# Turning q in 32x32 blocks on VectorE and scoring in 32x64 array tiles, in a fused low-rank attention and max-of-three FFN kernel

## Chip, cores and metric

One core of one Trainium2 chip runs the whole problem in one launch. The metric is the device time in microseconds of that core; three runs of the kernel before give a median of 399.84 us (399.8 to 400.65).

## What is computed

The inputs q, k, v are float32 of shape 8 x 8 x 1024 x 64 (batch, head, token, d); E and F are 64 x 1024. The FFN weights w1, w2, w3 are 512 x 768, w_out is 768 x 512. The output is float32, 8192 x 512.

```python
k_proj = np.einsum('ks,bhsd->bhkd', E, k)
v_proj = np.einsum('ks,bhsd->bhkd', F, v)
scores = np.matmul(q, k_proj.transpose(0, 1, 3, 2)) / np.sqrt(64)
scores = scores - np.max(scores, axis=-1, keepdims=True)
attn = np.exp(scores)
attn = attn / (np.sum(attn, axis=-1, keepdims=True) + 1e-09)
attn_out = np.matmul(attn, v_proj)
x = attn_out.transpose(0, 2, 1, 3).reshape(8 * 1024, 8 * 64)
h = np.maximum(np.maximum(x @ w1, x @ w2), x @ w3)
out = h @ w_out
```

The 1024 tokens are projected to 64 rows before the scores, so a score matrix is 1024 x 64 per head.

## The kernel before

Everything runs in bf16 with float32 sums. Token 8p + si of a batch lies in partition p at place si, so `q_t`, `k_t` and `v_t` are [128, head, 8, 64]. They are loaded with a cast by GpSimd's queue (`load`, L81), two buffers each.

The FFN works on half batches of 512 tokens (`ch`), 16 in all. One `l1` call (L176) is four matmuls of 128x128 by 512 columns into one of four rotating PSUM banks (0 to 3), and an eviction: ScalarE copies w1's product (L182), VectorE takes the maximum with w2's (L184) and with w3's (L186). So the same bank comes round four groups later, and the eviction of a group must be done by then. 18 such groups make one half batch; four `down` groups of six matmuls (L188) of the half batch before are put between them after groups 2, 5, 8 and 11.

The attention of the next batch is spread among these groups by a list of slots written out by hand: `attention` (L111) returns pairs of a slot number and a step, and `tick` (L457), called after every group, starts the steps that are due. In batches 2 to 7 the steps are: `kv` at slot 2 (the projections of k and v, 16 matmuls into bank 4), `scores(0)` at 10, `scores(1)` at 15, `sums` at 20, two reciprocals, and the two halves of the product with v at 25 and 30. For batch 1 the list is written out at L452, denser: `kv` at 20, `scores(0)` at 25, `scores(1)` at 28. Batch 0 has its own code and the change leaves its work alone.

The steps that matter here:

- After `kv`, the projected k is copied from PSUM to `kp2` twice over, once by ScalarE (L122) and once by VectorE (L123), so that a crossbar transpose on the Sync queue (L167) gives `kpT` with d in partitions 0 to 63 and again in 64 to 127. Two copies of the projected v follow on ScalarE (L125) and VectorE (L126). The four copies run one after another: each waits for the one before it on the other engine.
- q has to come with d on partitions too. For batches 2 to 7 two crossbar transposes per batch on the Sync queue do this (`q_turn`, L95): a partition of `qT` is (parity of the token, d). For batch 1 TensorE does it: `q_pe1` (L296), 32 transposes into PSUM and four copies out, at slots 22 and 24.
- `scores(u)` (L128) makes eight matmuls of 64 rows by 64 columns with 512 moving columns, four at a time in four 64x64 tiles of the array, and then two exponentials of 1024 elements per partition on ScalarE (L138).
- `load_behind_turn` (L89) lets GpSimd read one element of `kpT` before it issues the next loads, so the loads follow the turn of k.

Of the kernel before, what the change touches and what calls it, by code (L numbers as in the profile page):

```python
# [16 lines left out]
def kernel(ctx: ExitStack, tc: tile.TileContext, q, k, v, E, F, w1, w2, w3, w_out, out):  # L17
# [37 lines left out]
    xT = [T([P, NCT, 2, 512], BF16, f"xT{i}") for i in range(3)]  # L55
# [32 lines left out]

    def load_behind_turn(b, order="qkv"):  # L89

        nc.gpsimd.tensor_copy(out=seen, in_=kpT[(b - 1) % NB][:, 0, 0:1])
        for c in order:
            load(b, *{"q": (q, q_t), "k": (k, k_t), "v": (v, v_t)}[c])

    def q_turn(b, hs):  # L95
        nc.sync.dma_start_transpose(
            out=qT[b % NB][:, hs].rearrange("p h s t -> p (h s) t"),
            in_=q_t[b % NB][:, hs].rearrange("p h si d -> p (h si d)"),
        )


# [9 lines left out]
    def attention(b, turn):  # L111
        i = b % NB

        def kv():
            for si in range(SI):
                nc.tensor.matmul(out=ps[0:KP, AB, :], lhsT=eT[:, si, :], rhs=k_t[i][:, :, si, :],  # L116
                                 start=(si == 0), stop=(si == SI - 1))
                nc.tensor.matmul(out=ps[KP:P, AB, :], lhsT=fT[:, si, :], rhs=v_t[i][:, :, si, :],  # L118
                                 start=(si == 0), stop=(si == SI - 1))
            kv_k = ps[0:KP, AB, :].rearrange("p (h d) -> p h d", d=D)  # L120
            kv_v = ps[KP:P, AB, :].rearrange("p (g u dd f) -> p u g f dd", u=2, f=2, dd=HD)
            nc.scalar.copy(out=kp2[i][:, :, 0, :], in_=kv_k)  # L122
            nc.vector.tensor_copy(out=kp2[i][:, :, 1, :], in_=kv_k)  # L123
            turn(i)
            nc.scalar.copy(out=vp2[i][KP:P], in_=kv_v[:, 1])  # L125
            nc.vector.tensor_copy(out=vp2[i][0:KP], in_=kv_v[:, 0])  # L126

        def scores(u):  # L128
            for gg in range(2):
                g = 2 * u + gg  # L130
                for par in range(2):
                    r = slice(par * D, (par + 1) * D)
                    for col in range(2):
                        h = HEAD[2 * g + col]
                        nc.tensor.matmul(out=ps[col * KP:(col + 1) * KP, AB + 2 * gg + par, :],  # L135
                                         lhsT=kpT[i][r, h, :], rhs=qT[i][r, h, :, :], start=True, stop=True)
# [12 lines left out]
        def sums():  # L149
            quads(lambda rows, g: ones[rows, :])  # L150
            for u in range(2):
                nc.scalar.activation(out=lns[u], in_=ps[:, AB + 2 * u:AB + 2 * u + 2, :], func=AF.Ln)  # L152

        def recip(u):
            nc.scalar.activation(out=rinv[u], in_=lns[u], func=AF.Exp, scale=-1.0)  # L155

        def av(half):
            quads(lambda rows, g: vp2[i][rows, g, half, :])
            for u in range(2):
                nc.vector.tensor_tensor(out=xT[b % 3][:, 2 * u + half, :, :], in0=ps[:, AB + 2 * u:AB + 2 * u + 2, :],  # L160
                                        in1=rinv[u].rearrange("p (c n) -> p c n", c=2), op=ALU.mult)

        return [(2, kv), (10, lambda: scores(0)), (15, lambda: scores(1)), (20, sums),
                (21, lambda: recip(0)), (22, lambda: recip(1)), (25, lambda: av(0)), (30, lambda: av(1))]

    def turn_dma(i):
        nc.sync.dma_start_transpose(out=kpT[i], in_=kp2[i].rearrange("p h c d -> p (h c d)"))  # L167


    state = {"f": 0, "n": 0}  # L170
# [5 lines left out]
    def l1(b, ch, c, jt, i):  # L176
        bank = fbank()
        for ct in range(NCT):
            nc.tensor.matmul(out=ps[:, bank, :], lhsT=w_sb[i][:, ct, jt * P:(jt + 1) * P],  # L179
                             rhs=xT[b % 3][:, ct, ch, :], start=(ct == 0), stop=(ct == NCT - 1))  # L180
        if i == 0:
            nc.scalar.copy(out=h1s[jt % 2], in_=ps[:, bank, :])  # L182
        elif i == 1:
            nc.vector.tensor_tensor(out=m12[jt % 2], in0=ps[:, bank, :], in1=h1s[jt % 2], op=ALU.max)  # L184
        else:
            nc.vector.tensor_tensor(out=hT[c % 2][:, jt, :], in0=ps[:, bank, :], in1=m12[jt % 2], op=ALU.max)  # L186
# [45 lines left out]
    def k_proj0(g):  # L232
        for si in range(SI):
            for u in range(2):
                nc.tensor.matmul(out=ps[u * D:(u + 1) * D, 2, g * KP:(g + 1) * KP], lhsT=k_t[0][:, HEAD[2 * g + u], si, :],
                                 rhs=eT[:, si, :], start=(si == 0), stop=(si == SI - 1))
        nc.vector.tensor_copy(out=kpT[0][:, g, :], in_=ps[:, 2, g * KP:(g + 1) * KP])

    def v_proj0(g, bank):
        for si in range(SI):  # L240
# [5 lines left out]
    def scores0(ch, g, bank):  # L246
        for u in range(2):
            rows = slice(u * D, (u + 1) * D)
            nc.tensor.matmul(out=ps[u * KP:(u + 1) * KP, bank, :], lhsT=kpT[0][rows, g, :],  # L249
                             rhs=qT[0][rows, 4 * ch + g, :, :], start=True, stop=True)  # L250
# [21 lines left out]
    def q_up0():  # L272
# [4 lines left out]
                                     rhs=ident, start=True, stop=True)  # L277
        for j in range(2):
            (nc.vector.tensor_copy if j else nc.scalar.copy)(
                out=qT[0][:, 4 + 2 * j:6 + 2 * j].rearrange("p h s t -> p (h s t)"),  # L280
                in_=ps[:, 4 + 2 * j:6 + 2 * j, :].rearrange("p b n -> p (b n)"))

    def scores_up0():
# [5 lines left out]
    def av_up0():  # L289
# [6 lines left out]
    def q_pe1(hh):  # L296
        for h in range(4 * hh, 4 * hh + 4):
            for sp in range(SI // 2):
                o = (h % 2) * 512 + sp * P
                nc.tensor.transpose(out=psb[:, AB + (h % 4) // 2, o:o + P],  # L300
                                    in_=q_t[1][:, h, 2 * sp:2 * sp + 2, :].rearrange("p s d -> p (s d)"), identity=ident)
        for j in range(2):
            (nc.vector.tensor_copy if j else nc.scalar.copy)(
                out=qT[1][:, 4 * hh + 2 * j:4 * hh + 2 * j + 2].rearrange("p h s t -> p (h s t)"), in_=psb[:, AB + j, :])

    def warmup(n, bank):
        for _ in range(n):
# [47 lines left out]
    def q_turn0(g):  # L355
        for n in range(4):
            nc.tensor.transpose(out=psb[:, 4 + g, n * P:(n + 1) * P],
                                in_=q_0[:, n, 2 * g:2 * g + 2, :].rearrange("p h d -> p (h d)"), identity=ident)
        nc.vector.tensor_copy(out=qT[0][:, g].rearrange("p s t -> p (s t)"), in_=psb[:, 4 + g, 0:512])

    def q_cast0(g):
        if g > 1:
# [85 lines left out]
    for b in range(B):  # L448
        groups = attention(b + 1, turn_dma) if b + 1 < B else []
        if b == 0:  # L450
            g1 = [g for _, g in groups]
            groups = [(9, scores_up0), (12, lambda: sums0(1, 4)), (20, g1[0]), (22, lambda: q_pe1(0)), (24, lambda: q_pe1(1)), (25, g1[1]), (28, g1[2]),  # L452
                      (31, g1[3]), (32, g1[4]), (33, g1[5]), (34, g1[6]), (36, g1[7])]
        slot = 0
        gi = 0
# [1 line left out]
        def tick():  # L457
# [79 lines left out]
```

The softmax here doesn't subtract the row's maximum and nothing guards it: scores larger than these inputs give would overflow.

## Time and profile before

| what | value |
|---|---|
| three runs, median | 399.84 us |
| the profiled execution, its own time | 399.92 us |
| its span in the trace | 398.1 us |
| TensorE matmul busy | 392.5 us, 99% of the span |
| VectorE busy | 186.9 us, 47% |
| ScalarE busy | 166.0 us, 42% |
| GpSimd busy | 71.6 us, 18% |
| granted TensorE clock | 1.00 |
| mean DMA rate | 135 GB/s |
| crossbar transposes of q (L96) | 12 |
| crossbar transposes of k (L167) | 7 |

All times in the sections below are microseconds from the start of the span. The time of the profiled execution is 1.8 us longer than its span: the rest lies around the first and last instruction. A line such as "L123 DVE CAST kp<-ps 64x512" says source line, engine, operation, what is written from what, and partitions by elements; then come the count, the busy time, the mean in nanoseconds of one, and the idle time of the engine just before it with what ended that. Matmuls overlap in the array, so a matmul's mean time is a latency and not its share of the engine; what a group of matmuls costs is the distance between the starts of what stands before and behind it.

### The profile page before, as it was taken

What the parts mean: (1) busy time and instruction counts of PE and PEld (TensorE: products, weight loads), DVE (VectorE), ACT (ScalarE), POOL (GpSimd) and SP (SyncE); (2) the same over time, 40 slices, a digit from 0 to 9 for tenths busy, and PEclk for the clock granted to TensorE, in tenths of its full rate; (3) what the DMA queues carried; (4) which work ended last, traced back from release to release, by engine and by line L of the source; (5) the groups of instructions that cost most, each with busy time, mean ns of one, the idle gap of its engine ahead of it and who ended that gap; (6) DMA issues with size and microseconds to landing.
All of it is one profiled execution on the core that took longest, in us unless ns stands there. A gap on an engine that the chain in (4) does not pass through costs nothing.

```text
span 398.1 us, 6013 instructions
## 1 busy us (share of the span) xinstructions
PE 392.5 (99%) x2432; PEld 170.0 (43%) x2432; DVE 186.9 (47%) x269; ACT 166.0 (42%) x249; POOL 71.6 (18%) x110
## 2 busy tenths in 40 slices
PE   8999999999999999999999999999999999999996
PEld 4444443444444444444444444444444444444443
DVE  3347355453834365443843266342654338433441
ACT  3414457347225642347223662245522472222222
POOL 6452140150003300060000600033010000000000
PEclk9999999999999999999999999999999999999999
DMA  8999979999912998169920999129992111102022
GB/s 225 206 209 206 207 172 195 240 162 185 191 54 72 187 197 174 34 116 186 239 95 13 173 197 213 54 67 180 220 131 63 55 53 54 53 7 100 1 107 105
DMA packets 62667, 53.73 MB, mean 135 GB/s; under 512 B 30512, under 2 KB 57648, under 8 KB 62640
## 3 DMA queue, kind: packets, MB, share of 16 engines
q0 software_dynamic: 31776, 43.52, 53.8%
q1 hardware_dynamic: 30032, 8.92, 15.3%
q10 hardware_dynamic: 832, 0.92, 0.7%
q8 instruction: 19, 0.31, 0.3%
q14 instruction: 8, 0.07, 0.0%
HBM read 57.15 MB, written 16.78 MB: 186 GB/s over the span
## 4 chain that ended last, share of the span: by engine, by line
PE 95%; DMA 2%; DVE 1%; ACT 0%; POOL 0%; issue 0%; POOLq 0%; DVEq 0%
PE ps L179 59%; PE ps L203 19%; PE ps L116 3%; PE ps L145 3%; PE ps L407 2%; DMA k_t<-in_k_dram 2%; PE ps L135 2%; PE ps L398 1%; PE ps L216 1%; PE ps L308 1%; PE ps L229 1%; DVE xT L160 1%; PE ps L249 1%; PE ps L300 0%; PE ps L242 0%; PE ps L196 0%
## 5 line engine op out<-in xcount | busy, mean ns | idle before, releaser
L179 PE MATMUL ps<-xT,w_sb 128*128 128x512 bf16 x1080 | 246.3, 379 | 0.0
L179 PEld LDWEIGHTS <-w_sb 128*128 128x128 bf16 x1080 | 103.2, 98 | 132.1 <-issue 12.0
L184 DVE TENSOR_TENSOR m<-ps,h1s 128x512 f32<-128x512 f32 x90 | 62.2, 691 | 143.8 <-PE ps L179 124.5
L203 PE MATMUL ps<-wo_sb,hT 128*128 128x512 bf16 x354 | 85.5, 379 | 0.0
L182 ACT COPY h1s<-ps 128x512 f32<-128x512 f32 x90 | 52.8, 587 | 66.8 <-PE ps L179 66.5
L205 ACT COPY o_acc<-ps 128x512 f32<-128x512 f32 x59 | 34.6, 587 | 97.8 <-PE ps L203 97.8
L210 POOL DMA_DIRECT2D out_dram<-o_acc x28 | 20.1, 720 | 271.1 <-ACT o_acc L205 271.1
L186 DVE TENSOR_TENSOR hT<-ps,m 128x512 bf16<-128x512 f32 x90 | 62.3, 692 | 13.7 <-PE ps L179 5.2
L203 PEld LDWEIGHTS <-hT 128*128 128x128 bf16 x354 | 33.6, 98 | 44.1 <-issue 5.4
L160 DVE TENSOR_TENSOR xT<-ps,rinv 128x1024 bf16<-128x1024 f32 x28 | 32.9, 1218 | 7.8 <-PE ps L145 7.8
L138 ACT ACTIVATE pT<-ps 128x1024 bf16<-128x1024 f32 x28 | 27.1, 1022 | 13.3 <-PE ps L135 13.3
L87 POOL DMA_DIRECT2D v_t<-in_v_dram x21 | 15.3, 750 | 4.0 <-DMA q_t<-in_q_dram 2.0
L152 ACT ACTIVATE lns<-ps 128x1024 f32<-128x1024 f32 x14 | 13.6, 1022 | 1.9 <-PE ps L145 1.9
L155 ACT ACTIVATE rinv<-lns 128x1024 f32<-128x1024 f32 x14 | 14.2, 1061 | 0.0
L116 PE MATMUL ps<-k_t,eT 128*64 128x512 bf16 x56 | 13.4, 382 | 0.0
L118 PE MATMUL ps<-v_t,fT 128*64 128x512 bf16 x56 | 13.4, 382 | 0.0
L87 POOL DMA_DIRECT2D q_t<-in_q_dram x14 | 10.6, 767 | 3.2 <-DMA wo_sb<-in_moe_w_out_dram 1.1
L87 POOL DMA_DIRECT2D k_t<-in_k_dram x14 | 10.5, 762 | 2.2 <-ACT o_acc L445 1.2
L407 PE MATMUL ps<-xT,w_sb 128*128 128x512 bf16 x48 | 10.9, 379 | 0.0
L123 DVE CAST kp<-ps 64x512 bf16<-64x512 f32 x7 | 4.8, 683 | 12.6 <-ACT kp L122 12.6
L308 PE MATMUL ps<-warm 128*128 128x512 bf16 x26 | 9.4, 469 | 1.2 <-DVE ones L340 1.2
L122 ACT CAST kp<-ps 64x512 bf16<-64x512 f32 x7 | 4.1, 580 | 14.1 <-PE ps L118 14.1
(85 smaller groups left out, 155.5 us busy)
## 6 DMA issues: line engine op xcount, KB each, us to landing
out_dram<-o_acc POOLq DMA_DIRECT2D x30, 512.0 KB, 3.3
q_t<-in_q_dram POOLq DMA_DIRECT2D x15, 512.0 KB, 8.5
k_t<-in_k_dram POOLq DMA_DIRECT2D x14, 512.0 KB, 13.4
v_t<-in_v_dram POOLq DMA_DIRECT2D x18, 256.0 KB, 17.6
v_t<-in_v_dram POOLq DMA_DIRECT2D x7, 512.0 KB, 16.8
w_sb<-in_moe_w_dram POOLq DMA_DIRECT2D x4, 384.0 KB, 10.1
k_t<-in_k_dram POOLq DMA_DIRECT2D x4, 256.0 KB, 8.4
w_sb<-in_moe_w_dram POOLq DMA_DIRECT2D x4, 192.0 KB, 9.6
```

The costliest lines, as they stand in the source:

```text
L87: nc.gpsimd.dma_start(out=dst[b % NB][:, slots], in_=sv[:, heads])
L116: nc.tensor.matmul(out=ps[0:KP, AB, :], lhsT=eT[:, si, :], rhs=k_t[i][:, :, si, :], start=(si == 0), stop=(si == SI - 1))
L138: nc.scalar.activation(out=pT[:, 2 * u + gg, :, :], in_=ps[:, AB + 2 * gg:AB + 2 * gg + 2, :], func=AF.Exp, scale=scale)
L160: nc.vector.tensor_tensor(out=xT[b % 3][:, 2 * u + half, :, :], in0=ps[:, AB + 2 * u:AB + 2 * u + 2, :], in1=rinv[u].rearrange("p (c n) -> ...
L179: nc.tensor.matmul(out=ps[:, bank, :], lhsT=w_sb[i][:, ct, jt * P:(jt + 1) * P], rhs=xT[b % 3][:, ct, ch, :], start=(ct == 0), stop=(ct == ...
L182: nc.scalar.copy(out=h1s[jt % 2], in_=ps[:, bank, :])
L184: nc.vector.tensor_tensor(out=m12[jt % 2], in0=ps[:, bank, :], in1=h1s[jt % 2], op=ALU.max)
L186: nc.vector.tensor_tensor(out=hT[c % 2][:, jt, :], in0=ps[:, bank, :], in1=m12[jt % 2], op=ALU.max)
L203: nc.tensor.matmul(out=ps[:, bank, :], lhsT=hT[c % 2][:, jt, tt * P:(tt + 1) * P], rhs=wo_sb[:, jt, :], start=(jt == 0), stop=(jt == NJT - 1))
L205: nc.scalar.copy(out=o[:, tt, :], in_=ps[:, bank, :])
L210: nc.gpsimd.dma_start(out=dst[:, tt - 1:tt + 1, :], in_=o[:, tt - 1:tt + 1, :])
L407: nc.tensor.matmul(out=ps[:, bank, :], lhsT=w_sb[i][:, ct, jt * P:(jt + 1) * P], rhs=xT[0][:, ct, 0, :], start=(ct == 0), stop=(ct == NCT ...
```

## The change

q of batches 1 to 7 is turned by VectorE: `q_flip(b, g)` transposes two heads in 32x32 blocks, with two neighbouring bf16 values of d taken as one float32 word, [128, 512] words at a time, four calls per batch. Within a band of 32 partitions this puts the pair of d on the partition, and leaves the token in its band: partition 32r + j holds d pair j of the tokens of band r, with the two halves of the pair (f) side by side along the row.

The scores follow from that: for each pair of heads, 16 matmuls of 32 rows (d pairs of one band) by 64 columns with 256 moving columns, in eight 32x64 tiles at once, two passes f = 0 and 1 summed in PSUM; the moving operand steps over every second bf16 value. Four banks (one per band) hold 256 columns of each head pair. `kpT` becomes [128, head, f, 64] with the 32 d pairs repeated in the four bands, so `kp2` is filled with four repeats: ScalarE copies heads 0 to 3 and VectorE heads 4 to 7, 64 x 1024 elements each, and the crossbar transpose of k is twice as large. Neither the crossbar nor TensorE turns q of batches 1 to 7 any more. The exponential writes its result in token order, so the output's rows are addressed with a partition holding four neighbouring tokens per half batch. `xT` has two buffers in place of three.

```diff
-    qT = [T([P, H, SI // 2, P], BF16, f"qT{i}") for i in range(NB)]
-    kp2 = [T([KP, H, 2, D], BF16, f"kp2_{i}") for i in range(NB)]
-    kpT = [T([P, H, KP], BF16, f"kpT{i}") for i in range(NB)]
+    qT = [T([P, H, SI * D], BF16, f"qT{i}") for i in range(NB)]
+    kp2 = [T([KP, H, 2, 4, D // 2], BF16, f"kp2_{i}") for i in range(NB)]
+    kpT = [T([P, H, 2, KP], BF16, f"kpT{i}") for i in range(NB)]
...
-    out_v = out.rearrange("(b p sp par) m -> b par p sp m", p=P, sp=SI // 2, par=2)
+    out_v = out.rearrange("(b p ch t) m -> b ch p t m", p=P, ch=2, t=4)
...
-    def q_turn(b, hs):
-        nc.sync.dma_start_transpose(
-            out=qT[b % NB][:, hs].rearrange("p h s t -> p (h s) t"),
-            in_=q_t[b % NB][:, hs].rearrange("p h si d -> p (h si d)"),
+    def q_flip(b, g):
+        hs = slice(2 * g, 2 * g + 2)
+        nc.vector.transpose(
+            out=qT[b % NB][:, hs].bitcast(FP32).rearrange("p h n -> p (h n)"),
+            in_=q_t[b % NB][:, hs].rearrange("p h si d -> p (h si d)").bitcast(FP32),
         )
...
-            kv_k = ps[0:KP, AB, :].rearrange("p (h d) -> p h d", d=D)
+            kv_k = ps[0:KP, AB, :].rearrange("p (h dd f) -> p h dd f", dd=HD, f=2)
...
-            nc.scalar.copy(out=kp2[i][:, :, 0, :], in_=kv_k)
-            nc.vector.tensor_copy(out=kp2[i][:, :, 1, :], in_=kv_k)
+            for r in range(2):
+                (nc.vector.tensor_copy if r else nc.scalar.copy)(
+                    out=kp2[i].rearrange("k h f r dd -> k h r dd f")[:, 4 * r:4 * r + 4],
+                    in_=kv_k[:, 4 * r:4 * r + 4, None].to_broadcast([KP, 4, 4, HD, 2]))
...
-                for par in range(2):
-                    r = slice(par * D, (par + 1) * D)
-                    for col in range(2):
-                        h = HEAD[2 * g + col]
-                        nc.tensor.matmul(out=ps[col * KP:(col + 1) * KP, AB + 2 * gg + par, :],
-                                         lhsT=kpT[i][r, h, :], rhs=qT[i][r, h, :, :], start=True, stop=True)
+                for f in range(2):
+                    for r in range(4):
+                        rows = slice(r * HD, (r + 1) * HD)
+                        for col in range(2):
+                            h = HEAD[2 * g + col]
+                            nc.tensor.matmul(out=ps[col * KP:(col + 1) * KP, AB + r, gg * 256:(gg + 1) * 256],
+                                             lhsT=kpT[i][rows, h, f, :],
+                                             rhs=qT[i][rows, h].rearrange("p (n f) -> p n f", f=2)[:, :, f],
+                                             start=(f == 0), stop=(f == 1), tile_position=(r * HD, col * KP))
             for gg in range(2):
-                nc.scalar.activation(out=pT[:, 2 * u + gg, :, :], in_=ps[:, AB + 2 * gg:AB + 2 * gg + 2, :],
-                                     func=AF.Exp, scale=scale)
+                nc.scalar.activation(
+                    out=pT[:, 2 * u + gg].rearrange("p ch (t r n) -> p r (ch t) n", t=4, r=4),
+                    in_=ps[:, AB:AB + 4, gg * 256:(gg + 1) * 256].rearrange("p r (si n) -> p r si n", si=SI),
+                    func=AF.Exp, scale=scale)
...
-            groups = [(9, scores_up0), (12, lambda: sums0(1, 4)), (20, g1[0]), (22, lambda: q_pe1(0)), (24, lambda: q_pe1(1)), (25, g1[1]), (28, g1[2]),
+            groups = [(9, scores_up0), (12, lambda: sums0(1, 4)), (20, g1[0]),
+                      (22, lambda: q_flip(1, 0)), (23, lambda: q_flip(1, 1)), (25, g1[1]), (26, lambda: q_flip(1, 2)),
+                      (27, lambda: q_flip(1, 3)), (28, g1[2]),
                       (31, g1[3]), (32, g1[4]), (33, g1[5]), (34, g1[6]), (36, g1[7])]
...
-                if slot == 28:
-                    q_turn(2, slice(0, H // 2))
                 return
-            if b == 1 and slot == 3:
-                q_turn(2, slice(H // 2, H))
+            if b == 1 and slot in (4, 5, 6, 7):
+                q_flip(2, slot - 4)
             if b + 2 < B:
                 if slot == 9:
                     load_behind_turn(b + 2)
-                if slot == 18:
-                    q_turn(b + 2, slice(0, H // 2))
-                if slot == 27:
-                    q_turn(b + 2, slice(H // 2, H))
+                if slot in (32, 34, 36, 38):
+                    q_flip(b + 2, slot // 2 - 16)
```

More of the change, by code (lines that the diff above doesn't have):

```diff
@@ L49 @@
     q_t = [T([P, H, SI, D], BF16, f"q_t{i}") for i in range(NB)]
-    qT = [T([P, H, SI // 2, P], BF16, f"qT{i}") for i in range(NB)]
-    kp2 = [T([KP, H, 2, D], BF16, f"kp2_{i}") for i in range(NB)]
-    kpT = [T([P, H, KP], BF16, f"kpT{i}") for i in range(NB)]
+    qT = [T([P, H, SI * D], BF16, f"qT{i}") for i in range(NB)]
+    kp2 = [T([KP, H, 2, 4, D // 2], BF16, f"kp2_{i}") for i in range(NB)]
+    kpT = [T([P, H, 2, KP], BF16, f"kpT{i}") for i in range(NB)]
     vp2 = [T([P, NPAIR, 2, D // 2], BF16, f"vp2_{i}") for i in range(NB)]
     pT = T([P, NPAIR, 2, 512], BF16, "pT")
-    xT = [T([P, NCT, 2, 512], BF16, f"xT{i}") for i in range(3)]
+    xT = [T([P, NCT, 2, 512], BF16, f"xT{i}") for i in range(2)]
     lns = [T([P, 1024], FP32, f"lns{i}") for i in range(2)]
@@ L89, in load_behind_turn @@
     def load_behind_turn(b, order="qkv"):
-        nc.gpsimd.tensor_copy(out=seen, in_=kpT[(b - 1) % NB][:, 0, 0:1])
+        nc.gpsimd.tensor_copy(out=seen, in_=kpT[(b - 1) % NB][:, 0, 0, 0:1])
         for c in order:
             load(b, *{"q": (q, q_t), "k": (k, k_t), "v": (v, v_t)}[c])
-    def q_turn(b, hs):
-        nc.sync.dma_start_transpose(
-            out=qT[b % NB][:, hs].rearrange("p h s t -> p (h s) t"),
-            in_=q_t[b % NB][:, hs].rearrange("p h si d -> p (h si d)"),
+    def q_flip(b, g):
[3 more added lines that the diff above has]
+            in_=q_t[b % NB][:, hs].rearrange("p h si d -> p (h si d)").bitcast(FP32),
         )
@@ L159, in av @@
             for u in range(2):
-                nc.vector.tensor_tensor(out=xT[b % 3][:, 2 * u + half, :, :], in0=ps[:, AB + 2 * u:AB + 2 * u + 2, :],
+                nc.vector.tensor_tensor(out=xT[b % 2][:, 2 * u + half, :, :], in0=ps[:, AB + 2 * u:AB + 2 * u + 2, :],
                                         in1=rinv[u].rearrange("p (c n) -> p c n", c=2), op=ALU.mult)
@@ L166, in turn_dma @@
     def turn_dma(i):
-        nc.sync.dma_start_transpose(out=kpT[i], in_=kp2[i].rearrange("p h c d -> p (h c d)"))
+        nc.sync.dma_start_transpose(out=kpT[i].rearrange("p h f k -> p (h f) k"), in_=kp2[i].rearrange("k h f r dd -> k (h f r dd)"))
     state = {"f": 0, "n": 0}
@@ L179, in l1 @@
             nc.tensor.matmul(out=ps[:, bank, :], lhsT=w_sb[i][:, ct, jt * P:(jt + 1) * P],
-                             rhs=xT[b % 3][:, ct, ch, :], start=(ct == 0), stop=(ct == NCT - 1))
+                             rhs=xT[b % 2][:, ct, ch, :], start=(ct == 0), stop=(ct == NCT - 1))
         if i == 0:
@@ L236, in k_proj0 @@
                                  rhs=eT[:, si, :], start=(si == 0), stop=(si == SI - 1))
-        nc.vector.tensor_copy(out=kpT[0][:, g, :], in_=ps[:, 2, g * KP:(g + 1) * KP])
+        nc.vector.tensor_copy(out=kpT[0][:, g, 0, :], in_=ps[:, 2, g * KP:(g + 1) * KP])
     def v_proj0(g, bank):
@@ L248, in scores0 @@
             rows = slice(u * D, (u + 1) * D)
-            nc.tensor.matmul(out=ps[u * KP:(u + 1) * KP, bank, :], lhsT=kpT[0][rows, g, :],
-                             rhs=qT[0][rows, 4 * ch + g, :, :], start=True, stop=True)
+            nc.tensor.matmul(out=ps[u * KP:(u + 1) * KP, bank, :], lhsT=kpT[0][rows, g, 0, :],
+                             rhs=qT[0][rows, 4 * ch + g, :], start=True, stop=True)
     def exp0(ch, g, bank):
@@ L279, in q_up0 @@
             (nc.vector.tensor_copy if j else nc.scalar.copy)(
-                out=qT[0][:, 4 + 2 * j:6 + 2 * j].rearrange("p h s t -> p (h s t)"),
+                out=qT[0][:, 4 + 2 * j:6 + 2 * j].rearrange("p h n -> p (h n)"),
                 in_=ps[:, 4 + 2 * j:6 + 2 * j, :].rearrange("p b n -> p (b n)"))
@@ L293, in av_up0 @@
         norm0(1, 1, 4, (0, 1))
[L296 to L304, printed above, removed]
     def warmup(n, bank):
@@ L358, in q_turn0 @@
                                 in_=q_0[:, n, 2 * g:2 * g + 2, :].rearrange("p h d -> p (h d)"), identity=ident)
-        nc.vector.tensor_copy(out=qT[0][:, g].rearrange("p s t -> p (s t)"), in_=psb[:, 4 + g, 0:512])
+        nc.vector.tensor_copy(out=qT[0][:, g], in_=psb[:, 4 + g, 0:512])
     def q_cast0(g):
```

## Prediction, before the changed kernel ran

> **What bounds the kernel now.** I read the page first, for the engine that is always busy and the chain that ended last; its second line of part 2 and the chain's engine line:
>
> ```profile
> PE   8999999999999999999999999999999999999996
> ...
> PE 95%; DMA 2%; DVE 1%; ACT 0%; POOL 0%; issue 0%; POOLq 0%; DVEq 0%
> ```
>
> From slice 2 to the last but one TensorE never rests, and it is 95% of the chain. So a microsecond on TensorE counts whole, and one elsewhere counts only if TensorE comes to wait for it. Next the groups by form (count, busy us, mean ns, idle before):
>
> ```profile
> L135 PE MATMUL ps<-qT,kpT 64*64 64x512 bf16 x112 | 8.8, 388 | 0.0
> L123 DVE CAST kp<-ps 64x512 bf16<-64x512 f32 x7 | 4.8, 683 | 12.6 <-ACT kp L122 12.6
> L122 ACT CAST kp<-ps 64x512 bf16<-64x512 f32 x7 | 4.1, 580 | 14.1 <-PE ps L118 14.1
> L300 PE MATMUL ps<-ident,q_t 128*128 128x128 bf16 x32 | 2.1, 219 | 0.4 <-DVE vp L126 0.4
> ```
>
> L123 waits for L122, not for TensorE: the copies of k are one chain. Third, the chain in order of time where batch 1 is prepared (start, us, what):
>
> ```profile
> 49.74 0.59 ACT kp L122
> 50.34 0.02 issue
> 50.36 0.69 DVE kp L123
> 51.05 0.02 issue
> 51.08 0.38 ACT vp L125
> 51.45 0.02 issue
> 51.48 0.44 DVE vp L126
> 51.91 0.04 issue
> 51.95 1.05 PE ps L300 x16
> 53.01 1.73 PE ps L179 x8
> 54.73 0.89 PE ps L300 x16
> 55.63 0.86 PE ps L179 x4
> 56.49 0.56 PE ps L135 x8
> ```
>
> This is the one place where TensorE turns q, and it waits here for the copies. Fourth, the timeline behind `kv` of a later batch (start, us, engine):
>
> ```profile
> 165.05 0.58 ACT L122 CAST kp<-ps 64x512 bf16<-64x512 f32 x1 [2.15 <-PE ps L118]
> 165.67 0.68 DVE L123 CAST kp<-ps 64x512 bf16<-64x512 f32 x1 [1.73 <-ACT kp L122]
> 166.38 0.37 ACT L125 CAST vp<-ps 64x256 bf16<-64x256 f32 x1 [0.75 <-DVE kp L123]
> 166.78 0.43 DVE L126 CAST vp<-ps 64x256 bf16<-64x256 f32 x1 [0.43 <-ACT vp L125]
> ...
> 167.24 0.69 DVE L186 TENSOR_TENSOR hT<-ps,m 128x512 bf16<-128x512 f32 x1
> ```
>
> VectorE's eviction L186 stands behind the four copies and ends at 167.93. Its bank is taken again four groups later, by a group whose first matmul started at 168.81: 0.88 of slack. Last, the turns (duration min/median/max, ns):
>
> ```profile
> L96 SPq DMA_TRANSPOSE qT<-q_t x12: 2034/8246/10241, 71.9 to 283.1; - x12
> L167 SPq DMA_TRANSPOSE kpT<-kp x7: 1194/1196/1272, 51.1 to 306.5; - x7
> ```
>
> The crossbar turns of q run under full TensorE: nobody waits for them.
>
> **What the Trainium skill says.** Three places of the Trainium skill bear on this. "TensorE: Matmul & The Clock Gate", Part 3 (The mechanism): matmuls in different tiles start about 4 ns apart and run together. The trace agrees: four L135 starts lie 3 to 4 ns apart (172.793 to 172.803), the next four 0.240 later. "TensorEngine Tiling (Array Packing)", Key Properties: changing the tiling mode drains the array. The trace shows it: 0.309 in place of 0.216 between starts on entry, 0.308 on leaving. "SBUF — State Buffer" (SBUF cachelines): 16-byte lines are read at full rate with at least two hits each. The new moving operand, every second bf16, has four hits. The only strided moving operand before is L348 (284 to 328 ns against L235's 196): its weights are strided by 16 bytes as well. Their load takes 217 ns against 113, and a matmul ends 112 to 113 ns after its load in both lines, so I put the slowness on the weights. No run here separates the two.
>
> **The change, part by part.** All is summed against the profiled execution, 399.92 (span 398.1 and 1.8 around it), within 0.1 of the 399.84 median.
>
> *Scores, 14 groups, all on the path.* From the last matmul before a group to the first behind it is 0.867, against 0.216 between plain neighbours: a group costs 0.651. That is two switches of 0.093, two rounds of 0.216, and some 0.033 of first weights and spacing. After: 32 matmuls in eight tiles are four rounds of 256 columns. A round of 512 is 0.216 and one of 128 is 0.056 (the L300 starts), so 256 is 0.109: 4 x 0.109 + 0.186 + 0.05 = 0.67. The number of columns per tile, 1024, is unchanged. 14 x 0.02 = **+0.3**. Bounds: -0.2 if the spacing is hidden; +6.1 if the strided operand streams at half rate (0.109 more in each of 56 rounds).
>
> *Copies of k.* Each now covers 64x1024. ScalarE: L138 does 1024 from PSUM in 1022 ns, L122 does 512 in 580: +0.44. VectorE: L160 does 1024 from PSUM in 1218, L123 683: +0.54. The order of the built program keeps VectorE's copy waiting for ScalarE's, so the chain grows by 0.98. Against 0.88 of slack plus a few hundredths for the semaphore, TensorE stalls 0.16 in each of batches 3 to 7: **+0.8**. Scattered two-byte writes could double the copies (another 2.2 in each batch, +11 at most; I hold that unlikely, as L126 reads at a stride of two for no extra); zero if the slack just holds.
>
> *Batch 2, prepared in batch 1.* No `down` groups stand here, the slack is 0.5 (L186 ends 79.70, the bank is wanted at 80.21): a stall of 0.48. Four transposes at slots 4 to 7 then stand before L184 and L186. A transpose of 128x512 words is unknown: nearest row L343, a cast of 128x512 SBUF to SBUF, 628 ns; I take 0.65, and 1.2 as the upper bound (half rate). Group 9 of that half batch (counted from 0, as all here) then waits 0.2 for its bank. **+0.7** (0 to 2.5).
>
> *Batch 1.* Removed: 32 transposes x 0.056 = 1.79, and the wait before them, 51.37 to 51.95, 0.58; two copies of 1.01 on ScalarE and two of 0.69 on VectorE. Without them TensorE would reach `scores(0)` at 54.1. But VectorE now has: k copy to 52.0, v copy to 52.9, L184 to 53.6, L186 to 54.3, two transposes to 55.7. Group 8 waits 0.5 for L184's bank, and `scores(0)` for the second transpose. The turn of k, twice as large, starts at 52.05; L167 lands 2.6 after its issue, 3.6 in batch 1. The q turn of the same 16 blocks issues in 2.03, 0.84 longer, and lands 5.0 after. I take 3.4 (2.6 to 5.2): kpT at 55.5. So `scores(0)` starts at 55.7 against 56.42 before, -0.7; at slots 26 and 27 the last transpose ends near 59.5 where the second half of `scores(1)` wants it at 59.15, +0.35. Net **-0.4** (-1.3 to +1.6).
>
> *At nothing:* the transposes at slots 32 to 38. VectorE has 1.4 of evictions in 3.9 there, 2.7 with two transposes; the banks keep about one us of slack, even at 1.2 each. Removing 12 crossbar turns frees the Sync queue, which had nothing urgent behind them. The larger turn of k has from 167.35 to 172.8 for its 3.4; GpSimd's loads behind it (L91) keep their slot. q of batch 2 landed at 74.3; a us later is still before VectorE's first transpose near 80.7. The exponential stays at 1024 elements; output packets only grow.
>
> Sum: 399.92 + 0.3 + 0.8 + 0.7 - 0.4 = **401.3**.
>
> **Rivals.** (a) *Faster.* The turn of q on TensorE in batch 1 is the only TensorE work that goes. Its price is 2.37; it decides if kpT and two transposes are there by 54.6 and the slack behind `kv` holds: then 399.92 - 2.37 + 0.5 + 0.3 = 398.4. Against it: VectorE's own queue, 55.7 by the rows above. (b) *Cancel.* The slack of 0.88 just covers the copies and batch 2's transposes are short: 399.92 + 0.3 + 0.3 - 0.4 = 400.1. (c) *Strided operand at half rate:* 401.3 + 6.1 = 407.4; for it L348's slowness, against it the equal distance from load to end. (d) *VectorE's transposes at half rate:* batch 1 to +1.1, batch 2 to +2.2: 404.3. That the change doesn't do what it says is excluded by the built program: no q turn on Sync or TensorE is left, 28 transposes stand on VectorE.
>
> **How the numbers follow.** Forecast 0.45 (400.7 to 403); (a) 0.13; (b) 0.17; (c) 0.12; (d) 0.13. Same means within 0.2%, 0.8 us, about what a measurement of this kernel tells from no change. Faster is (a), 0.13; same (b), 0.17; slower the rest, 0.70. The range 398.9 to 405.5 leaves out (c), the far part of (a) and the doubled copies. The forecast's own range lies inside.
>
> **What would show it.** The start-to-start cost of a scores group: 0.67, and its rounds 0.109; 0.22 would be (c). Means of the two copies of k: 1.02 and 1.22. Means of the transposes: 0.65. TensorE waiting for VectorE's L186 behind each `kv` by 0.1 to 0.2, 0.5 in batch 1. `scores(0)` of batch 1 near 55.7, with the DVE transpose as the last to arrive. I am wrong if the copies overlap, if the turn of k takes over 4, or if a group costs over 0.8.

## The result, and the profile after

| kernel | median, us | range, us |
|---|---|---|
| before | 400.02 | 399.8 to 400.65 |
| changed | 465.72 | 464.5 to 466.24, and once 560.19 |

The changed kernel takes 1.1634 times as long as the one before (95% interval 1.1601 to 1.1666): 66 us more, where 1.4 were forecast and the range ended at 405.5. One of its four executions ran at a mean granted clock of 0.73 and took 560.19 us, so the median above is of the other three, at 0.94, and the profile shown here is of a further execution of the same kernel, at 465.38 us (span 463.6).

The page first, in the order in which the prediction read it: TensorE's busy tenths and its granted clock in 40 slices, and the engines' shares of the chain that ended last.

```profile
PE   8999579579993999859997599957999489999996
...
PEclk9999869979997999959999799996999979999999
...
PE 78%; DVE 10%; ACT 8%; DMA 2%; issue 1%; POOL 0%; DVEq 0%; POOLq 0%
```

TensorE was solid from slice 2 on; now it has seven holes of one or two slices, and the clock falls in the same places. VectorE and ScalarE, 1% of the chain before, are 18% of it. The groups by form (count, busy us, mean ns, idle before) name the lines:

```profile
L126 DVE CAST kp<-ps 64x1024 bf16<-64x1024 f32 x7 | 32.6, 4657 | 41.3 <-ACT kp L126 41.3
L126 ACT CAST kp<-ps 64x1024 bf16<-64x1024 f32 x7 | 32.8, 4686 | 14.2 <-PE ps L121 14.2
L99 DVE STREAM_TRANSPOSE qT<-q_t 128x512 f32<-128x512 f32 x28 | 19.3, 695 | 0.0
```

The two copies of k take 4.66 and 4.69 us each, against 0.68 and 0.58 before. The turn of q, the new operation, has 0.695. The waits of TensorE (engine, line, what it waited for: us in total, times, longest):

```profile
PE ps L189 <- DVE hT L196: 43.8, 6, 7.5
PE ps L189 <- DVE m L194: 7.5, 1, 7.5
```

That is 51.3 us, one wait in each of the seven batches that are prepared beside the FFN. L189 and L196 are the matmul and the eviction that were L179 and L186 before. The timeline behind `kv` of one batch shows what the eviction stood behind:

```profile
135.73 4.69 ACT L126 CAST kp<-ps 64x1024 bf16<-64x1024 f32 x1 [2.15 <-PE ps L121]
...
140.45 4.66 DVE L126 CAST kp<-ps 64x1024 bf16<-64x1024 f32 x1 [5.83 <-ACT kp L126]
145.14 0.37 ACT L130 CAST vp<-ps 64x256 bf16<-64x256 f32 x1 [4.72 <-DVE kp L126]
...
145.54 0.42 DVE L131 CAST vp<-ps 64x256 bf16<-64x256 f32 x1 [0.43 <-ACT vp L130]
145.99 0.69 DVE L196 TENSOR_TENSOR hT<-ps,m 128x512 bf16<-128x512 f32 x1
...
146.74 1.86 PE L189 MATMUL ps<-xT,w_sb 128*128 128x512 bf16 x4 [7.09 <-DVE hT L196]
```

It is the chain that the prediction drew: ScalarE's copy, VectorE's copy, the two copies of v, then L196, whose bank TensorE needs. Only it now takes 10.95, from 135.73 to 146.68, where it took 2.88. The last line holds a second loss: four matmuls of L189 in 1.86 us, where four of L179 took 1.04 in the kernel before, at full clock:

```profile
164.92 1.04 PE L179 MATMUL ps<-xT,w_sb 128*128 128x512 bf16 x4
```

The busy times of each engine by stretch say so too (stretch; us; PE, PEld, DVE, ACT, POOL busy; PEclk; DMA share; GB/s):

```profile
140.00:147.00 7.00, 0.26 (x1) 0.10 (x1) 6.09 (x4) 1.85 (x4) 0.00 (x0) 0.77 0.09 14
147.00:154.00 7.00, 6.95 (x53) 2.79 (x53) 1.71 (x3) 1.82 (x3) 1.40 (x3) 0.74 0.33 87
```

In the first stretch TensorE does nothing until 146.74. In the second it is busy throughout, at a mean clock of 0.74: (1 - 0.74) x 7 / 0.5 = 3.6 us of it at half.

### The profile page after: what moved, and what is told of

It reads as the page before. It is cut to its first block, busy times and chain, and to the rows that moved or that the text cites. A ratio compares the mean times of both kernels' runs of the same rounds, so it can differ in the third digit from the quotient of the medians.

```text
span 558.2 us, 6574 instructions
## 1 busy us (share of the span) xinstructions
PE 504.7 (90%) x2686; PEld 197.5 (35%) x2736; DVE 229.9 (41%) x295; ACT 192.6 (34%) x247; POOL 66.5 (12%) x110
## 4 chain that ended last, share of the span: by engine, by line
PE 84%; DVE 8%; ACT 6%; issue 1%; DVEq 0%
PE ps L189 51%; PE ps L213 17%; ACT kp L126 6%; DVE kp L126 6%; PE ps L119 3%; PE ps L155 2%; PE ps L406 2%; PE ps L141 2%; PE ps L307 2%; PE ps L226 1%; PE ps L397 1%; DVE hT L196 1%; DVE vp L131 1%; PE ps L239 1%; PE ps L259 0%
## 5 line engine op out<-in xcount | busy, mean ns | idle before, releaser
L189 PE MATMUL ps<-xT,w_sb 128*128 128x512 bf16 x1043 | 320.2, 467 | 47.0 <-DVE hT L196 37.1
L189 PEld LDWEIGHTS <-w_sb 128*128 128x128 bf16 x1080 | 120.1, 113 | 232.5 <-issue 230.9
L194 DVE TENSOR_TENSOR m<-ps,h1s 128x512 f32<-128x512 f32 x90 | 62.1, 691 | 194.6 <-PE ps L189 187.1
L213 PE MATMUL ps<-wo_sb,hT 128*128 128x512 bf16 x348 | 113.0, 475 | 0.8 <-issue 0.2
L196 DVE TENSOR_TENSOR hT<-ps,m 128x512 bf16<-128x512 f32 x90 | 61.8, 686 | 35.4 <-PE ps L189 34.9
L220 POOL DMA_DIRECT2D out_dram<-o_acc x28 | 15.2, 544 | 406.0 <-ACT o_acc L215 394.6
L213 PEld LDWEIGHTS <-hT 128*128 128x128 bf16 x354 | 39.9, 116 | 63.6 <-issue 63.2
L126 DVE CAST kp<-ps 64x1024 bf16<-64x1024 f32 x7 | 32.6, 4658 | 45.2 <-ACT kp L126 45.2
L126 ACT CAST kp<-ps 64x1024 bf16<-64x1024 f32 x7 | 32.8, 4687 | 19.0 <-PE ps L121 19.0
L99 DVE STREAM_TRANSPOSE qT<-q_t 128x512 f32<-128x512 f32 x28 | 19.3, 694 | 0.0
L119 PE MATMUL ps<-k_t,eT 128*64 128x512 bf16 x56 | 16.8, 454 | 0.0
L121 PE MATMUL ps<-v_t,fT 128*64 128x512 bf16 x56 | 16.7, 455 | 0.0
L165 ACT ACTIVATE rinv<-lns 128x1024 f32<-128x1024 f32 x14 | 14.2, 1060 | 0.0
L406 PE MATMUL ps<-xT,w_sb 128*128 128x512 bf16 x46 | 13.7, 462 | 0.3 <-issue 0.2
## 6 DMA issues: line engine op xcount, KB each, us to landing
w_sb<-in_moe_w_dram POOLq DMA_DIRECT2D x4, 384.0 KB, 10.2
```

The costliest lines, as they stand in the source:

```text
L126: (nc.vector.tensor_copy if r else nc.scalar.copy)(out=kp2[i].rearrange("k h f r dd -> k h r dd f")[:, 4 * r:4 * r + 4], in_=kv_k[:, 4 * r ...
L213: nc.tensor.matmul(out=ps[:, bank, :], lhsT=hT[c % 2][:, jt, tt * P:(tt + 1) * P], rhs=wo_sb[:, jt, :], start=(jt == 0), stop=(jt == NJT - 1))
```

## The experiments

Two things were open: why a copy of 1024 values takes 4.7 us, and whether anything else in the change costs time. The first idea was the order in which the copy writes. Its result has f (the parity of d) outside dd, but it walks through its input in the order of the input, with f innermost; so consecutive two-byte values go to and fro between two places 256 bytes apart.

### e1_rows: the same copies, written in rows

Number of values, fourfold repeat, source and engines stay; only the walk changes, so that the write runs on and the read from PSUM jumps.

```diff
-                    out=kp2[i].rearrange("k h f r dd -> k h r dd f")[:, 4 * r:4 * r + 4],
-                    in_=kv_k[:, 4 * r:4 * r + 4, None].to_broadcast([KP, 4, 4, HD, 2]))
+                    out=kp2[i][:, 4 * r:4 * r + 4],
+                    in_=kv_k[:, 4 * r:4 * r + 4].rearrange("p h dd f -> p h f dd")[:, :, :, None].to_broadcast([KP, 4, 2, 4, HD]))
```

> The changed kernel with one thing altered: the two copies of k write kp2 row by row (h, f, r, dd, contiguous) and read PSUM at a stride of two, instead of the other way round. Theory A (the cost lies in writes of single bf16 values that jump 256 bytes to and fro): both copies fall from 4.68 and 4.66 us to about 1.02 and 1.22, the stall behind kv to some 0.2, the TensorE clock stays granted, and the time is that of the prediction's own sum, about 401.3. Theory B (the fourfold repeated read, a step of zero, is what is slow): the copies stay at 4.7 us and the time near 466. Theory C (the eight-tile scores or VectorE's transposes also cost much): copies fast, time still well above 403.

Measured: 402.25 us (401.97 to 402.5) beside 400.07 of the kernel before on the same chip, 1.0046 (1.0029 to 1.0064). The groups by form and the waits of TensorE:

```profile
L126 DVE CAST kp<-ps 64x1024 bf16<-64x1024 f32 x7 | 8.5, 1216 | 15.5 <-ACT kp L126 15.5
L126 ACT CAST kp<-ps 64x1024 bf16<-64x1024 f32 x7 | 7.0, 1006 | 14.2 <-PE ps L121 14.2
```

```profile
PE ps L189 <- DVE hT L196: 1.1, 5, 0.4
PE ps L141 <- DMA kpT<-kp: 1.0, 1, 1.0
PE ps L141 <- DVE qT L99: 0.8, 1, 0.8
PE ps L189 <- DVE m L194: 0.4, 1, 0.4
```

The copies fall to 1.22 and 1.01 us, the 51.3 us behind `kv` to 1.5, the clock stays at 1.00, and 63 of the 65 us between the two kernels are gone. This edit changes the order of the write and that of the read together; e3_jump_in_before and e5_write_forms below tell the two apart, and it is the write. So the order of the write is the cause of all but 2.2 us, and this run shows the change with its copies at the price that the prediction had assumed.

### e4_after_again: the changed kernel once more

No edit; one execution with its profile, the one shown above.

> The changed kernel once more, for a profile at the same granted clock as the kernel before. 464 to 467 us; copies of 4.68 and 4.66 us, seven stalls of some 7 us behind kv, and the granted clock at one half for about 6.8 us after each.

Measured: 465.38 us, mean granted clock 0.937. The trace's clock records put seven stretches of half clock in it, one behind each long wait: four of 6.8 us and three of 10.2, each beginning while TensorE still waits.

### e2_warm: keep TensorE busy while it waits

The changed kernel, with 30 matmuls on zeros put where TensorE would wait, into bank 7, which stands free at that time.

```diff
-        return [(2, kv), (10, lambda: scores(0)), ...
+        return [(2, kv), (6, lambda: warmup(30, 7)), (10, lambda: scores(0)), ...
...
-            g1 = [g for _, g in groups]
+            g1 = [g for t, g in groups if t != 6]
...
-                      ..., (23, lambda: q_flip(1, 1)), (25, g1[1]), ...
+                      ..., (23, lambda: q_flip(1, 1)), (24, lambda: warmup(30, 7)), (25, g1[1]), ...
```

The last four lines concern batch 1's list, which has its filler at another slot.

> The changed kernel with 30 idle matmuls of zeros (30 x 0.216 = 6.5 us at full clock) into the free bank 7, placed just ahead of the group that stalls behind each kv, so that TensorE is busy while it would wait. The stall itself stays: 7 x about 7.1 us. Theory A (a part of the loss is the clock that is halved for 6.8 us after each idle stretch): the mean clock returns to 1.0 and the time is 400 + 7 x 7.1, about 450, some 16 us under the changed kernel. Theory B (the whole loss is waiting): no change, 466 or a little more.

Measured: 452.65 us (451.97 to 453.12), 1.1303 (1.1279 to 1.1327), clock 1.00 throughout. The wait on L196 that is left:

```profile
PE ps L189 <- DVE hT L196: 4.2, 6, 1.1
```

The filler takes 30 x 0.216 = 6.5 us in each of seven batches, 45.4, and does nothing useful; with the 3.8 us by which the waits on L196 and L194 exceed those of e1_rows (4.2 + 1.1 - 1.5) that is 49.2, near the 50.4 between this run and e1_rows. So this run pays for the waiting at full clock, and what the changed kernel takes beyond it, 465.38 - 452.65 = 12.7 us, is the halved clock. The clock records allow somewhat more: of the seven stretches 31.9 us lie behind the moment at which TensorE resumes, 3.6 to 6.0 each, and half of that is 15.9, if it were work without a gap. It is not: in batch 1 the slower work hides waits for k and q that are 1.8 us in e2_warm and 0.2 in the changed kernel.

### e3_jump_in_before: the jump alone, in the kernel before

The kernel before, with nothing of the change but a jumping write: its two copies of 512 values go to and fro over 64 bytes. This puts the d of k in another order within each head, so the scores are those of a permuted k.

```diff
-            nc.scalar.copy(out=kp2[i][:, :, 0, :], in_=kv_k)
-            nc.vector.tensor_copy(out=kp2[i][:, :, 1, :], in_=kv_k)
+            for c in range(2):
+                (nc.vector.tensor_copy if c else nc.scalar.copy)(
+                    out=kp2[i][:, :, c, :].rearrange("k h (f dd) -> k h dd f", f=2),
+                    in_=kv_k.rearrange("p h (dd f) -> p h dd f", f=2))
```

> The kernel before with only its two copies of k (64x512) altered to write single bf16 values that jump 64 bytes to and fro between two runs. This permutes d within k, so the scores are those of a permuted k; all else is as before. Theory A (jumping two-byte writes cost some 4.4 ns each, whatever the distance): copies of 2.4 us each in place of 0.58 and 0.68, the chain 3.5 us longer, less 0.88 of slack: 7 x about 2.7, 418 to 420. Theory B (it is the 256-byte distance or the repeat): copies unchanged, 400.

Measured: 430.07 us (428.86 to 430.72), 1.0737 (1.0712 to 1.0762), clock 0.975. The copies (min/median/max in ns, first and last start):

```profile
L123 ACT CAST kp<-ps x7: 2420/2436/2439, 49.7 to 331.3; 64x512 bf16<-64x512 f32 x7
L123 DVE CAST kp<-ps x7: 2415/2417/2425, 52.2 to 333.8; 64x512 bf16<-64x512 f32 x7
```

The price of the jump was forecast right, 2.4 us for 512 values, and it needs neither the repeat, nor the 1024 values, nor the new turn of q. The time was 10 us over the expectation. TensorE waits for 20.0 us in all (16.0 on L188 in six batches, 4.0 in batch 1's turn of q), against the expectation's 7 x 2.7 = 18.9; beside them the clock records have six stretches of 3.4 us at half clock, which lose up to 6 x 3.4 / 2 = 10.2. The expectation had left these out.

The seven waits were of 4.0, 3.0 and five times 2.6 us. Half clock came with six of them; with the first of 2.6 us it did not. These are the 3.41 us behind that wait, and the stretch at half clock behind the next (columns as above):

```profile
134.97:138.38 3.41, 3.41 (x16) 1.56 (x16) 1.28 (x2) 0.72 (x2) 0.17 (x1) 1.00 0.14 21
185.44:188.85 3.41, 3.41 (x10) 1.22 (x8) 0.69 (x1) 0.59 (x1) 0.03 (x1) 0.50 0.00 0
```

The clock records suggest why. In the traces of the kernel before and of the nine runs of this section all changes of the clock stand whole multiples of 3.413 us apart. Cut into stretches on that grid, these traces have no exception to the following: full clock gave way to half when TensorE had been idle for 2.12 us or more of the stretch just past, and stayed when it had been idle for 1.89 or less; half clock lasted another stretch after 0.85 us of idle time or more, and ended after 0.22 or less. The wait of 2.6 us that cost nothing more lay across a boundary of the grid, with 1.86 us on one side and 0.73 on the other. So the same wait can cost a stretch at half clock or none, by where it falls. This is read from the records; no run was made to test it.

### e5_write_forms: ten forms of the write, side by side

e1_rows, with ten more forms of copy into a scratch tile at the end of the kernel, each first on VectorE and then on ScalarE, one at a time; only their durations are of interest, and each is a single measurement. The second form as an example, and the loop:

```diff
+    s64 = scr[0:KP]
+    forms = [
...
+        (s64[:, 0:1024].rearrange("p (x f y) -> p x y f", f=2, y=128), src.rearrange("p (x y f) -> p x y f", f=2, y=128)),
...
+    for o, i_ in forms:
+        nc.vector.tensor_copy(out=o, in_=i_)
+        nc.scalar.copy(out=o, in_=i_)
```

> The row-wise kernel of e1 with twenty copies of 64x1024 float32 values from PSUM to bf16 in a scratch tile added behind the last group (they add to the time and change no output), each form on VectorE and on ScalarE, one at a time: (1) rows, (2) to and fro over 256 bytes, (3) over 64 bytes, (4) over 8 bytes, (5) every second value, 4 bytes apart, (6) every eighth, 16 bytes apart, (7) 64 values 256 bytes apart, (8) pairs of bf16 to and fro over 512 bytes, (9) float32 to and fro over 512 bytes, (10) as 2 but read from SBUF. Theory A (what costs is each jump to another place): 2, 3, 4, 8 halved, 9 near 4.7 us, 10 as 2; 6 near 4.7 too. Theory B (what costs is a two-byte write that leaves half a word): 5 as slow as 2, and 9 fast, about 1.2. Theory C (strided reads matter): 10 differs from 2.

Measured, in ns:

| form | values written in a row to the same 16 bytes | VectorE | ScalarE |
|---|---|---|---|
| 1: rows of bf16 | 8 | 1206 | 1006 |
| 2: to and fro over 256 bytes | 1 | 4658 | 4662 |
| 3: to and fro over 64 bytes | 1 | 4683 | 4687 |
| 4: to and fro over 8 bytes, inside 16 | 8 | 1217 | 1006 |
| 5: every second bf16 | 4 | 1283 | 1286 |
| 6: every eighth bf16, 16 bytes apart | 1 | 4672 | 4675 |
| 7: 64 values, 256 bytes apart | 1 | 434 | 436 |
| 8: pairs of bf16, to and fro over 512 bytes | 2 | 1218 | 1060 |
| 9: float32, to and fro over 512 bytes | 1 | 1910 | 1912 |
| 10: as 2, but read from SBUF as bf16 | 1 | 2731 | 4700 |

On VectorE's timeline (start, us), forms 6 to 9 look like this:

```profile
423.39 4.67 DVE L524 CAST scr<-ps 64x1024 bf16<-64x1024 f32 x1 [1.35 <-ACT scr L525]
432.80 0.43 DVE L524 CAST scr<-ps 64x64 bf16<-64x64 f32 x1 [4.74 <-ACT scr L525]
433.74 1.22 DVE L524 CAST scr<-ps 64x1024 bf16<-64x1024 f32 x1 [0.50 <-ACT scr L525]
436.08 1.91 DVE L524 COPY scr<-ps 64x1024 f32<-64x1024 f32 x1 [1.13 <-ACT scr L525]
```

None of the three theories of the expectation holds alone. If every move to other 16 bytes cost the same (A), form 9 would be as slow as form 2; if every lone two-byte value did (B), form 5 would be; and the source (C) makes a difference in form 10 on VectorE alone. What fits forms 1 to 9 is this: a write is at or near the rate of rows when at least two values in a row go to the same 16 bytes (the slowest is form 5 on ScalarE, 1286 against 1006). If only one does, a bf16 costs 4.4 ns on both engines ((4662 - 153) / 1024, where 153 is the fixed part that ScalarE's 579 ns for 512 and 1006 for 1024 leave) and a float32 about 1.7 ((1912 - 153) / 1024), and the distance of the jump does not matter (16, 64 or 256 bytes). One question is left open: a visit of two bf16 values in form 8 takes ScalarE (1060 - 153) / 512 = 1.8 ns, as long as a visit of one float32, so for jumps out of the 16 bytes it could as well be that four bytes at once are what counts, and not two values. Why VectorE is quicker than ScalarE in form 10 was not tried either.

### e6_k_once: take the repeats out of the chain

e1_rows, but ScalarE writes one of the four repeats (512 values) and VectorE fills the other three from SBUF, as float32 words of two bf16 each.

```diff
+            nc.scalar.copy(out=kp2[i][:, :, :, 0, :], in_=kv_k.rearrange("p h dd f -> p h f dd"))
+            kw = kp2[i].rearrange("k h f r dd -> k (h f) (r dd)").bitcast(FP32).rearrange("k x (r w) -> k x r w", r=4)
+            nc.vector.tensor_copy(out=kw[:, :, 1:4, :], in_=kw[:, :, 0:1, :].to_broadcast([KP, 16, 3, HD // 2]))
```

> The row-wise kernel of e1, but PSUM is read once for k: ScalarE writes one of the four repeats (64x512, runs of 64 bytes, about 0.58 us), and VectorE fills the other three from SBUF as float32 words (64x768, 0.5 to 0.9 us). Theory (the rest over the kernel before is the copy chain and batch 1): the waits of TensorE for VectorE behind kv vanish (1.5 us in e1), kpT of batch 1 lands about 1 us sooner, though the first two transposes of q then hold scores(0): 400.0 to 400.8. Rival (the rest is in the scores themselves, 14 times more than their 0.035): no change against e1, 402.2.

Measured: 400.69 us (400.38 to 400.96) beside 400.17, 1.0014 (1.0008 to 1.0021).

```profile
L127 DVE COPY kp<-kp 64x768 f32<-64x768 f32 x7 | 3.9, 552 | 12.6 <-ACT kp L125 12.6
```

ScalarE's copy takes 579 ns and VectorE's fill 552, less than the 683 of the kernel before, and no wait behind `kv` is left. The waits that are left are in batch 1: `scores(0)` waits 1.1 for the turn of k and `scores(1)` 0.8 for a turn of q.

### e7_k_once_q_early and e9_q_early_again: batch 1's turns of q earlier

e6_k_once, with the four VectorE transposes of batch 1 at slots 20 (ahead of `kv`), 21, 23 and 24. The second run repeats the first on another chip, beside e8.

```diff
-            groups = [..., (20, g1[0]), (22, lambda: q_flip(1, 0)), (23, lambda: q_flip(1, 1)), (25, g1[1]), (26, lambda: q_flip(1, 2)),
-                      (27, lambda: q_flip(1, 3)), (28, g1[2]),
+            groups = [..., (20, lambda: q_flip(1, 0)), (20, g1[0]), (21, lambda: q_flip(1, 1)),
+                      (23, lambda: q_flip(1, 2)), (24, lambda: q_flip(1, 3)), (25, g1[1]), (28, g1[2]),
```

> As e6, and the four transposes of batch 1 stand at slots 20 (ahead of the copies of k), 21, 23 and 24 in place of 22, 23, 26 and 27. scores(0) of batch 1 then waits only for kpT, near 54.4, and scores(1) for nothing: another 1.5 to 2 us, 398.3 to 399.3, faster than the kernel before by 0.2 to 0.4%. Rival (VectorE's evictions are only pushed back and TensorE waits for their banks instead): 400 to 401.

> The kernel of e7 unchanged, on the same chip as e8, to compare the two: 399.4 to 399.9.

Measured: 399.67 us (399.33 to 399.95) beside 400.17, 0.9989 (0.9982 to 0.9995), and on the second chip 399.77 (399.47 to 399.94) beside 400.33, 0.9985 (0.9978 to 0.9992). The wait for q is gone. The one for k stays, at 1.0 (1.5 in e9), and that is where the first expectation, 398.3 to 399.3, failed. From the chain in order of time in e7:

```profile
50.88 4.17 DMA kpT<-kp
55.05 0.04 issue
55.09 0.66 PE ps L140 x29
```

Issued earlier, at 50.88, the turn of k took 4.2 us to land and not 3.4, so that `scores(0)` still began at 55.09. In e1, e6, e7 and e9 it was issued between 50.61 and 51.81 and landed between 55.05 and 55.39 all the same, after 3.6 us for the latest issue and 4.6 for the earliest. What holds it back there was not tried.

### e8_before_k_once: the quick fill in the kernel before

The kernel before, with its own turn of q; only its second copy of k is filled from SBUF in float32 words.

```diff
-            nc.vector.tensor_copy(out=kp2[i][:, :, 1, :], in_=kv_k)
+            kw = kp2[i].rearrange("k h c d -> k h (c d)").bitcast(FP32)
+            nc.vector.tensor_copy(out=kw[:, :, HD:2 * HD], in_=kw[:, :, 0:HD])
```

> The kernel before, with q turned as before, but its second copy of k filled by VectorE from SBUF as float32 words (64x256, some 0.35 us) in place of a second read of PSUM. Theory (what e7 gains is in the copy chain and not in the new turn of q): the wait of 0.58 us ahead of batch 1's turn on TensorE all but vanishes, nothing else moves: 399.4 to 399.7, level with e7. Rival (the chain has slack everywhere but there, and the turn is then late by something else): 400.1, no change, and e7 keeps a gain of its own.

Measured: 399.51 us (398.97 to 400.15) beside 400.33, 0.9984 (0.9977 to 0.999). The fill takes 285 ns in place of 683, and in the chain in order of time the turn of q on TensorE (L301) follows the matmul groups without a wait:

```profile
49.52 1.83 PE ps L180 x8
51.35 0.89 PE ps L301 x16
```

On the same chip e9 gives 399.77. The new turn of q with a quick copy chain, and the old one with a quick copy chain, are level, 0.3 us or less apart: what is gained against 400.33 is gained by the copies, and the new turn of q brings no net gain that these runs can tell. The traces show that it is a balance and not an absence of effects. From the start of `kv` for batch 1 to that for batch 2 the kernel before takes 27.05 us, e8 26.48, e9 26.31 and e7 25.88. In each batch from 3 on, e7 and e9 take 46.77 us, and e8 and the kernel before 46.70. From the last matmul's end to the end of the span, all kernels with the new turn take 3.5 us in place of 3.3; why was not tried (the change also addresses the output's rows differently).

## Why the prediction was wrong

The failed step is the price in "Copies of k". It took 1.02 and 1.22 us from the rows L138 and L160, which move as many values but write them in rows, and it set the doubt aside in these words: "Scattered two-byte writes could double the copies (another 2.2 in each batch, +11 at most; I hold that unlikely, as L126 reads at a stride of two for no extra)". Three things are wrong with that. The reason given concerns a read of PSUM, and says nothing of a write to SBUF; e1_rows reads in jumps and writes in rows and pays nothing. The bound was no bound: the two copies took 9.34 us together, not 2 x 2.24 = 4.5. And the range left even that bound out, though no row of the kernel before had such a write.

One step ahead of it, the prediction had the rule in hand. It cites the Trainium skill, "SBUF — State Buffer", note on SBUF cachelines: lines of 16 bytes, and at least two hits in each, one after the other, for full bandwidth. It asked that of the operand that TensorE reads, found four hits, and never asked it of the copy's result, which has one before it jumps. e5_write_forms agrees with the page: two or more hits in a row are at full rate, or within 30% of it in form 5 on ScalarE (1286 against 1006), one is not. The page gives no size for the penalty; here it made a write of bf16 4.6 times as long on ScalarE.

With the measured price the prediction's own working gives the waits. The chain of the two copies grows from 1.30 us (165.05 to 166.35 in its timeline) to 9.38 (135.73 to 145.11), by 8.1; less the slack of 0.88 that is 7.2, and the waits are 7.1 to 7.5. Seven times 7.2 is 50.4, near the 51.3 us of waits in the trace. By as much, 50.4, e2_warm exceeds e1_rows; but e1_rows still waits for 1.5, so no more should be read into the equal figures than that they are near.

The second failure is a term that was not there: the clock. The Trainium skill, "TensorE: Matmul & The Clock Gate", Part 1, says that TensorE falls to half clock after an idle window of about 3.4 us. Half clock does come with the waits of 7 us in the changed kernel and of 2.6 to 4.0 in e3, in stretches of 3.4, 6.8 or 10.2 us. But a whole idle window was not needed: 2.12 us of idle time in 3.41 were enough in e3. The prediction's small stalls, up to 0.5, were under that, and e9 with a wait of 1.5 kept 1.00. But a doubled copy was thinkable, and its price was not only its wait.

The whole difference, 465.38 - 400.07 = 65.3 us, is thus, taken as steps from run to run, 50.4 of waiting (e2_warm less e1_rows), 12.7 of halved clock (the changed kernel less e2_warm), and 2.2 of everything else (e1_rows less the kernel before). That last part is what the forecast was about, and e1_rows shows it, point by point:

- Sum: 401.3 forecast for the kernel with copies at 1.02 and 1.22; 402.25 measured with copies at 1.01 and 1.22, in the forecast's own range of 400.7 to 403.
- Scores: 0.67 a group forecast; 0.683 to 0.693 measured, with rounds of 0.114 to 0.139 where 0.109 was forecast. 14 x 0.035 = +0.5 instead of +0.3. Rival (c), the strided operand at half rate, is false.
- Waits behind `kv`: 0.16 a batch forecast, 0.2 measured in four of five; 0.4 in batch 2, forecast 0.48 plus a later 0.2 that did not show. Near.
- VectorE's transposes: 0.65 forecast, 0.695 measured. Rival (d), 1.2, is false.
- Batch 1: the turn of k was to land in 3.4 and took 3.6; `scores(0)` at 55.7 forecast, 55.43 measured. But the last to arrive was k, not q as forecast, and the second half of `scores(1)` waited 0.8 for q, not 0.35. The gain of 0.4 did not come: batch 1, from its `kv` to the next, took 27.41 in place of 27.05.
- Rival (a), faster because the TensorE turn goes, did not happen: it wanted k and q there by 54.6, and the turn of k lands after 55, even in e7, where nothing of q is late.
- Rival (b), the effects cancel because the copies fit into their slack, needed quicker copies: with these, e6_k_once is 0.5 us above the kernel before and e7 0.5 below it.

The trace of e1_rows is 1.9 us longer than that of the kernel before. By the starts of `kv`, it reaches its first one 0.2 sooner, and takes longer by 0.4 in batch 1, 0.6 in batch 2, nearly 0.2 in each of the five batches after that, and 0.3 behind the last matmul, a term that the prediction did not have. So batch 1 has the wrong sign, and that the sum of 401.3 comes as near to 402.25 as it does is not because every term was right.

## What to carry to other kernels

Of a copy that reorders, look at the order in which it writes, and count how many values in a row fall into the same 16 bytes; if it is one, walk the other way, with the jump on the PSUM side, or write once and fill repeats from SBUF in words of four bytes. An eviction chain with 0.9 us of slack turned such a copy into a stall of the whole engine, and at stalls of 2.6 us and more the clock added to it, in six cases of seven in e3. A doubt that no row of the profile can settle belongs inside the range, at the size of the worst form.

## What the runs showed of the hardware that was not expected

- A lone bf16 written to its 16 bytes cost 4.4 ns on VectorE and ScalarE alike when it was read from PSUM; a lone float32 cost about 1.7. So 1024 values in pairs of bf16 over a jump of 512 bytes (1218 and 1060 ns) are nearly as fast as rows (1206 and 1006).
- A read of PSUM in jumps of two float32 costs nothing in a copy: 1006 and 1216 ns in e1_rows against 1006 and 1206 in rows.
- VectorE fills 768 float32 words from SBUF in 552 ns and 256 in 285, so repeats are cheaper filled from SBUF than taken again from PSUM (683 ns for 512 bf16).
- The moving operand of every second bf16 runs in eight 32x64 tiles at about 0.114 us for 256 columns, near the 0.108 that dense operands would take by the 0.216 for 512 in the kernel before.
- In these traces the clock changed on a grid of 3.413 us, and it fell by TensorE's idle time within one stretch of that grid (2.12 us was enough, 1.89 was not), not by the length of a wait as such.
